# Opening of an attention and gated feed-forward kernel: fewer unread transposes, a later weight load, crossed value loads, an early SiLU table

## The chip, the core and the metric

The kernel runs on one core of a Trainium2 chip. The metric is the device time of one execution in microseconds (us), lower is better. The engines are TensorE (PE, with its weight loads PEld), VectorE (DVE), ScalarE (ACT), GpSimd (POOL) and SyncE (SP), whose queue issues nearly all loads and stores.

## What is computed

`q`, `k`, `v` are 8 batches x 8 heads x 576 rows x 64 columns in float32. Attention runs inside chunks of 64 rows; its result, 4608 tokens x 512, goes through a gated feed-forward layer with 1536 inner columns.

```python
scores = scale * np.matmul(q_c, k_c.transpose(0, 1, 2, 4, 3))   # chunks of 64 x 64
attn = np.exp(scores - max); attn = attn / (sum + 1e-09)
x = (attn @ v_c) as 4608 x 512
g = x @ w_gate
out = (silu(g) * (x @ w_val)) @ w_out
```

## The kernel before, in words

The 4608 tokens are nine blocks of 512. Products in the feed-forward part are made of three passes: each operand is split into a high part (`fp32r`) and a rest, and low x high, high x low and high x high are added in PSUM. The weights are split on the way in: a float64-looking pair of words (`raw`) is turned into `t` by ACT (`scale`, line 84, and `below`, line 91) and DVE (`shift`, `power`, `weigh`, `join`, lines 87 to 102), and then into `w` by `upper` (ACT) and `lower` (DVE). `Up(f)` does so for 128 gate and 128 value columns, `Out(f)` for 128 rows of `w_out`; `wo_raw`, `woh` and `wol` are the latter's results. Up to f = 11 the weights are split while two blocks (0 and 1) are worked on; from block 2 on they are there.

The opening, some 47 us, is attention of blocks 0 and 1, the splitting of weights 0, 1 and 2, and the first feed-forward products. Its order on PE, ACT and DVE is a table of steps written out by hand (`opening`, lines 630 to 637), and no engine departs from its order. A step of attention is a letter, a block, and a head pair or couple: `S` scores (line 228), `M` maxima and `K` their two parts, `B` subtracts the maxima in PSUM by two matmuls (line 585), `E` exponents (line 589), `Z`, `R`, `N` sums, inverses, scaling, `T` transposes on PE (line 392), `C` copies their result to `pT` on ACT (line 608), `X` multiplies by the values (line 406), `U` and `L` split the result into `xh` and `xl`. `G` and `V` are single matmuls of the first products (line 416); `H0` is the SiLU of the first one on ACT (line 434) and `Q0` its product with the other on DVE (line 441). `gs`, `vs`, `w1s`, `w2s` and so on are steps of the weights: `w2s` is `scale` of `Up(2)`. `.6` is six transposes of the identity into a tile that nobody reads (`keep_warm`, line 60); 15 more stand ahead of the table.

The values are needed in two forms: the even head pair of a couple as loaded, the odd one with the two halves of 64 partitions exchanged. `exchange` (line 349) makes the latter on POOL from a loaded tile, for both blocks.

Loads are issued by SP in the order of the program text (lines 507 to 521). A tile of the pool `const` has a tag; two tiles of one tag share their place, so a load into it waits for the last reader of the tile before. A load also waits until the eighth load ahead of it has landed, since its semaphore is used in turn by eight. SP is in order: what is behind a waiting load waits too.

```python
    up[2].load()
    down[0].load()
    values = []
    for a, vs in ((a0, v0), (a1, v1)):
        for c in range(2):
            pool, tag = (ld, "v_t") if a is a0 else (wp, ("woh", "wol")[c])
            odd = pool.tile([P, 2 * T, C], F32, name="v_t", tag=tag)
            a.exchange(vs[c][:, 1], odd)
```

Of the kernel before, what the change touches and what calls it, by code (L numbers as in the profile page):

```python
# [8 lines left out]
F32 = mybir.dt.float32  # L9
# [6 lines left out]
AF = mybir.ActivationFunctionType  # L16
# [3 lines left out]
P = 128  # L20
C = 64
# [6 lines left out]
NP = H // 2  # L28
T = 4
# [6 lines left out]
def attn_then_gated_ffn(ctx: ExitStack, tc: tile.TileContext, qk, v, wgv, wo, out):  # L36
    nc = tc.nc
    const = ctx.enter_context(tc.tile_pool(name="const", bufs=1))
    ld = ctx.enter_context(tc.tile_pool(name="ld", bufs=2))
    one = ctx.enter_context(tc.tile_pool(name="one", bufs=1))  # L40
    wp = ctx.enter_context(tc.tile_pool(name="wp", bufs=2))
    hp = ctx.enter_context(tc.tile_pool(name="hp", bufs=2))
    xs = ctx.enter_context(tc.tile_pool(name="xs", bufs=2))
    small = ctx.enter_context(tc.tile_pool(name="small", bufs=2))
# [6 lines left out]
    ident = const.tile([P, P], F32, name="ident")  # L51
# [4 lines left out]
    def keep_warm(n):  # L56

        ps = ps_gv.tile([P, P], F32, name="unread", tag="ps_gv")
        for _ in range(n):
            nc.tensor.transpose(ps, ident, ident)  # L60
# [44 lines left out]
    class Up(Narrow):  # L105
# [12 lines left out]
        def load(self):  # L118
            f = self.f
            self.raw = const.tile([P, 2 * DM], U64, name="raw", tag=self.at())  # L120
            nc.sync.dma_start(out=self.raw, in_=wgv[f].rearrange("p g n -> p (g n)"))
# [45 lines left out]
    class Out(Narrow):  # L167
# [6 lines left out]
        def load(self):  # L174
            f = self.f
            if f % 2 == 0:
                pool, tag = (const, "w7") if f == 0 else (one, "s_sb")
                Out.raw = pool.tile([P, 2, DM], U64, name="raw", tag=tag)
                nc.sync.dma_start(out=Out.raw, in_=wo[f * P:(f + 2) * P, :].rearrange("(n p) m -> p n m", p=P))
            self.mine = Out.raw[:, f % 2]  # L180
# [144 lines left out]
    class First(Attn):  # L325
# [18 lines left out]
        def load_v(self, p, t):  # L344
            nc.sync.dma_start(out=t, in_=v[:, p:p + t.shape[1], self.b])  # L345

        def exchange(self, t, to):
            for h in range(2):
                nc.gpsimd.tensor_copy(out=to[h * C:(h + 1) * C], in_=t[(1 - h) * C:(2 - h) * C])
# [82 lines left out]
    def silu(pg):  # L432
        h = hp.tile([P, N], F32, name="h")
        nc.scalar.activation(h, pg, AF.Silu, scale=2.0 ** -8)  # L434
        return h
# [4 lines left out]
    def times(h, pv):  # L440
        nc.vector.scalar_tensor_tensor(out=h, in0=pv, scalar=2.0 ** -8, in1=h, op0=ALU.mult, op1=ALU.mult)  # L441
# [49 lines left out]
    up, down = [Up(f) for f in range(NF)], [Out(f) for f in range(NF)]  # L491
# [12 lines left out]
    a0, a1 = First(0), First(1)  # L504
# [2 lines left out]
    w, o = up[0], down[0]  # L507
    q0 = [a0.load_qk(0), a0.load_qk(1)]
    wg = Half(w, 0)
    q0 = q0, [a0.load_qk(2, 2, const, "w4")]  # L510
    v0 = const.tile([P, NP, 2 * T, C], F32, name="v_t", tag="w3")
    v0 = [v0[:, p:p + 2] for p in (0, 2)]
    for p in (0, 2):
        a0.load_v(p, v0[p // 2])
# [2 lines left out]
    up[1].load()  # L517
    v1 = [ld.tile([P, 2, 2 * T, C], F32, name="v_t", tag="qk_t") for _ in range(2)]
    for p in (0, 2):
        a1.load_v(p, v1[p // 2])  # L520
    up[2].load()
    down[0].load()
    values = []
    for a, vs in ((a0, v0), (a1, v1)):
        for c in range(2):
            pool, tag = (ld, "v_t") if a is a0 else (wp, ("woh", "wol")[c])
            odd = pool.tile([P, 2 * T, C], F32, name="v_t", tag=tag)
            a.exchange(vs[c][:, 1], odd)
            values.append((vs[c][:, 0], odd))

    def x_of(a, p):
        return [x[:, p % 2] for x in a.x[p // 2]]
# [87 lines left out]
    for a, qs in ((a0, q0[0] + q0[1]), (a1, q1[0] + q1[1])):  # L620
# [6 lines left out]
    weights = {"g": wg, "v": wv, "w1": up[1], "w2": up[2]}  # L627


    opening = """  # L630
        gs S00 S01 .4 M001 M000 K00 gh gp B000 B001 .6 gb S02 gw S03 .6 E000 gj Z000 E001 Z001 M010 M011 K01 R00
        B010 gu B011 .6 N00 E010 E011 Z010 vs Z011 vb T00 vh T01 .6 S11 R01 N01 S10 T02 C00 T03 C01 gl M100 S13
        C03 M101 S12 vp K10 vw B100 B101 C02 vj X01 M111 E100 E101 M110 vu Z100 K11 X00 Z101 w1s U03 vl R10 B111
        U00 U01 L03 E111 B110 G0_31 N10 V0_31 V0_02 G0_01 V0_32 E110 U02 G0_32 L01 Z110 V0_11 Z111 G0_30 L02
        G0_11 w1b R11 V0_01 T11 L00 N11 T10 G0_10 C10 V0_10 w1h G0_21 G0_22 G0_02 V0_21 G0_12 w2s V0_22 V0_30
        V0_20 V0_00 G0_20 V0_12 G0_00 C11 H0 T12 T13 C12 C13 X10 w1p Q0 U11 X11 U10 U12 w1w U13 w1j L10 L11 L12
        L13 w1u
    """
# [1 line left out]
    for do in opening.split():  # L640
        if do[0] == ".":
            keep_warm(int(do[1:]))
        elif do[0] in "gvw":
            getattr(weights[do[:-1]], steps[do[-1]])()
        elif do[0] in "GV":
            if do[0] not in products:
                products[do[0]] = Product(a0, 0, "GV".index(do[0]))
            products[do[0]].add((int(do[3]), int(do[4])))
        elif do == "H0":
            h0 = silu(products["G"].ps)  # L650
        elif do == "Q0":
            times(h0, products["V"].ps)
        else:
            b, i = int(do[1]), int(do[2])
            pairs = do[0] in "STCUL"
            getattr(couples[b, i // 2 if pairs else i], do[0])(i if pairs else int(do[3:] or 0))
# [65 lines left out]
    f, o = NF - 1, down[NF - 1]  # L722
# [6 lines left out]
    nxt = First(2)  # L729
# [17 lines left out]
    z, two, px = {}, {}, {}  # L747
# [4 lines left out]
    def load_v():  # L752
        for p in range(NP):
            two[p] = (hp if p % 2 else ld).tile([P, 2 * T, C], F32, name="v_t", tag="o_sb" if p % 2 else "v_t")
            if p % 2 == 0:
                nc.sync.dma_start(out=two[p], in_=v[:, p, nxt.b])
            else:
                for h in range(2):
                    r, to = slice(h * C, (h + 1) * C), slice((1 - h) * C, (2 - h) * C)
                    nc.sync.dma_start(out=two[p][to], in_=v[r, p, nxt.b])  # L760

    def turn():
        nxt.turned = const.tile([P, NP, N], F32, name="pT", tag="turned")
# [19 lines left out]
    def rest(p):  # L783
        for i in (p, p + 1):
# [4 lines left out]

    extra = {0: lambda: nxt.exponents(0), 1: lambda: (nxt.exponents(2), sums(0)), 2: lambda: nxt.normalize(0, z[0]),  # L790
             3: lambda: (sums(2), load_v()), 4: lambda: nxt.normalize(2, z[2]), 6: turn, 7: lambda: copy(2),
             8: columns, 9: lambda: (first(2), rest(0)), 10: lambda: rest(2)}
    for f in range(NF):
# [5 lines left out]
    def block(a, b):  # L799
        nxt = Attn(b + 1) if b + 1 < NB else None  # L800
        middle, behind = {}, {}
        if nxt:


            kept_v = []

            def scores():
                tiles = [nxt.load_qk(0), nxt.load_qk(1)], [nxt.load_qk(2, 2, const, "turned")]
                ps = nxt.products(tiles[0], pool=ps_gv, tag="ps_gv"), nxt.products(tiles[1])
                nxt.less_top(nxt.take(ps[0], 0), 0)  # L810
                nxt.less_top(ps[1], 2)

            def load_v():
                kept_v.extend(nxt.load_v_crossed(p, "v_t" if p < 2 else "qk_t") for p in range(NP))

            def values():
                nxt.columns_crossed(kept_v[:2], 0, 2, ps_gv, "ps_gv")
                nxt.columns_crossed(kept_v[2:], 2, 2)

            middle = {3: lambda: nxt.exponents(0, NP)}  # L820
            behind = {1: scores, 3: lambda: nxt.normalize(0, NP), 4: lambda: nxt.turn(0, 0), 5: lambda: nxt.turn(0, 1),
                      6: lambda: (nxt.turn(2, 0), load_v()), 7: lambda: nxt.turn(2, 1),
                      8: values, 9: lambda: nxt.ready(0, 2), 10: lambda: nxt.ready(2, 2)}
        for f in range(NF):
            wo_f = []

            def between():
                middle.get(f, lambda: None)()
                wo_f.extend(out_weights(f))

            h = gated(a, f)
            between()
            lag(parts(a, f, h), wo_f)
            behind.get(f, lambda: None)()
        return nxt

    a = nxt
    for b in range(2, NB):
        a = block(a, b)
# [34 lines left out]
```

## Time and profile before

| | |
|---|---|
| median of 3 runs | 952.28 us (952.1 to 952.45) |
| the profiled execution's own time | 952.15 us |
| its span, first to last instruction | 950.4 us |
| busy share of the span | PE 99%, PEld 82%, DVE 51%, ACT 35%, POOL 1% |
| granted TensorE clock | 1.000 of full speed (the level of 2.4 GHz) |
| matmuls | 6299 |

The span is 1.75 us shorter than the time of that execution; the rest lies around it. The page gives busy shares over the whole span, and PE is busy in nearly all of it, so the places where PE is idle are few and lie at the start: its first slice of 23.8 us shows 7 tenths, all later ones 9 or more except the last.

### The profile page before, as it was taken

The numbers are of one execution on the slowest core, as the hardware profiler recorded it, in microseconds if no ns is written. First come the engines' busy times: TensorE is split into PE (matmuls) and PEld (weight loads), VectorE is DVE, ScalarE is ACT, GpSimd is POOL, SyncE is SP. The second block draws the span as 40 slices with busy tenths as digits, with TensorE's granted clock in tenths as the row PEclk, the third lists the DMA queues.
The fourth block names the chain that finished last, engine by engine and source line by source line (L and its number), as shares of the span: only waits on it lengthen the run. The fifth ranks groups of instructions, "written<-read, shape, count | busy, mean of one in ns | idle before, by whom it ended". The sixth has DMA issues, their size and how long they took to land.

```text
span 950.4 us, 14625 instructions
## 1 busy us (share of the span) xinstructions
PE 940.5 (99%) x6299; PEld 778.6 (82%) x6299; DVE 480.4 (51%) x792; ACT 336.3 (35%) x540; POOL 7.0 (1%) x14
## 2 busy tenths in 40 slices
PE   7999999999999999999999999999999999999998
PEld 6888888888888888888888888888888888888886
DVE  7966666574475336632574337533663256432222
ACT  4745444354332333133323233233423342332222
POOL 1100000000000000000000000000000000000000
PEclk9999999999999999999999999999999999999999
DMA  9614332443300230022102030023002210000001
GB/s 363 228 54 155 155 111 99 156 167 112 89 1 1 89 87 3 1 90 67 23 0 90 1 90 1 5 84 90 1 1 89 67 23 1 1 16 29 1 1 44
DMA packets 43936, 63.85 MB, mean 67 GB/s; under 512 B 27488, under 2 KB 27744, under 8 KB 42464
## 3 DMA queue, kind: packets, MB, share of 16 engines
q1 hardware_dynamic: 42144, 59.78, 18.3%
q10 hardware_dynamic: 1728, 3.15, 0.9%
q8 instruction: 49, 0.80, 0.3%
q14 instruction: 15, 0.12, 0.0%
HBM read 50.33 MB, written 12.58 MB: 66 GB/s over the span
## 4 chain that ended last, share of the span: by engine, by line
PE 97%; DMA 2%; SPq 0%; issue 0%; ACT 0%; DVE 0%
PE ps_gv L416 62%; PE ps_o L460 10%; PE ps_o L462 10%; PE ps_o L461 10%; PE ps_a L228 2%; DMA qk_t<-in_qk 2%; PE ps_a L306 1%; PE ps_a L406 1%; PE ps_a L585 0%; PE ps_a L392 0%; DMA out<-o_sb 0%; PE pt L392 0%; SPq L200 0%; SPq L154 0%; SPq L345 0%
## 5 line engine op out<-in xcount | busy, mean ns | idle before, releaser
L416 PE MATMUL ps_gv<-xh,w 128*128 128x512 f32 x1728 | 531.0, 389 | 0.0
L416 PEld LDWEIGHTS ps_gv<-xh,w 128*128 128x128 f32 x1728 | 324.3, 188 | 67.4 <-ACT xh L535 0.2
L416 PE MATMUL ps_gv<-xl,w 128*128 128x512 f32 x864 | 336.1, 391 | 0.0
L441 DVE SCALAR_TENSOR_TENSOR h<-ps_gv,h 128x512 f32<-128x512 f32 x108 | 74.6, 691 | 365.1 <-PE ps_gv L416 357.8
L416 PEld LDWEIGHTS ps_gv<-xl,w 128*128 128x128 f32 x864 | 162.1, 188 | 34.6 <-issue 0.4
L434 ACT ACTIVATE h<-ps_gv 128x512 f32<-128x512 f32 x108 | 64.6, 598 | 313.0 <-PE ps_gv L416 313.0
L460 PE MATMUL ps_o<-woh,hl 128*128 128x512 f32 x432 | 168.4, 390 | 0.0
L461 PE MATMUL ps_o<-wol,hh 128*128 128x512 f32 x432 | 168.1, 389 | 0.0
L462 PE MATMUL ps_o<-woh,hh 128*128 128x512 f32 x432 | 168.1, 389 | 0.0
L64 ACT CAST hh<-h 128x512 fp32r<-128x512 f32 x96 | 59.6, 620 | 182.7 <-DVE h L441 182.7
L461 PEld LDWEIGHTS ps_o<-wol,hh 128*128 128x128 f32 x432 | 81.1, 188 | 16.9
L460 PEld LDWEIGHTS ps_o<-woh,hl 128*128 128x128 f32 x432 | 81.1, 188 | 16.9
L462 PEld LDWEIGHTS ps_o<-woh,hh 128*128 128x128 f32 x432 | 81.1, 188 | 16.8
L293 DVE STREAM_TRANSPOSE turned<-s_sb 32x256 f32<-32x256 f32 x192 | 83.7, 436 | 2.7
L65 DVE TENSOR_TENSOR wol<-wo,woh 128x512 fp32r<-128x512 f32 x108 | 73.8, 684 | 12.7 <-ACT woh L64 12.6
L65 DVE TENSOR_TENSOR hl<-h,hh 128x512 fp32r<-128x512 f32 x96 | 66.4, 692 | 18.1 <-ACT hh L64 11.1
L64 ACT CAST woh<-wo 128x512 fp32r<-128x512 f32 x108 | 66.1, 612 | 15.9 <-DVE wo L102 15.9
L228 PEld LDWEIGHTS ps_a<-qk_t 64*64 64x64 f32 x1152 | 18.0, 135 | 5.4 <-issue 3.4
L228 PE MATMUL ps_a<-qk_t 64*64 64x64 f32 x1152 | 19.8, 220 | 1.6 <-DMA qk_t<-in_qk 1.6
L99 DVE TENSOR_TENSOR t<-t 128x1024 bf16<-128x1024 bf16 (+1 forms) x13 | 8.5, 650 | 22.1 <-ACT t L91 21.9
L475 ACT ACTIVATE o_sb<-ps_o 128x512 f32<-128x512 f32 (+1 forms) x36 | 18.6, 593 | 2.2 <-PE ps_o L462 2.0
L136 ACT CAST w<-t 128x1024 fp32r<-128x1024 f32 x11 | 11.6, 1054 | 16.7 <-DVE t L102 16.7
(70 smaller groups left out, 409.1 us busy)
## 6 DMA issues: line engine op xcount, KB each, us to landing
raw<-in_wgv SPq DMA_DIRECT2D x11, 1024.0 KB, 7.0
qk_t<-in_qk SPq DMA_DIRECT2D x10, 1024.0 KB, 7.5
out<-o_sb SPq DMA_DIRECT2D x35, 256.0 KB, 2.3
qk_t<-in_qk SPq DMA_DIRECT2D x16, 512.0 KB, 4.0
raw<-in_wo SPq DMA_DIRECT2D x6, 1024.0 KB, 4.9
v_t<-in_v SPq DMA_DIRECT2D x28, 128.0 KB, 2.7
h<-h ACTq DMA_DIRECT2D x12, 256.0 KB, 2.0
h_in<-h SPq DMA_DIRECT2D x6, 512.0 KB, 3.5
```

Of the source, the lines that this page charges most:

```text
L64: nc.scalar.copy(out=hi, in_=src)
L65: (engine or nc.vector).tensor_tensor(out=lo, in0=src, in1=hi.bitcast(F32), op=ALU.subtract)
L136: nc.scalar.copy(out=self.w[:, 0], in_=self.t)
L228: nc.tensor.matmul(ps[h][j * C:(j + 1) * C, i, u // 2, :], part[:, us:us + C], part[:, M * P + us:M * P + us + C], start=not more or first ...
L293: nc.vector.transpose(out=self.turned[to:to + 32, p:p + 2, j, :, 32 * (i % 2):32 * (i % 2) + 32], in_=src[32 * i:32 * i + 32, :, o // 2, 3 ...
L416: nc.tensor.matmul(ps, w, x, start=first and (k, i) == which[0], stop=last and (k, i) == which[-1])
L434: nc.scalar.activation(h, pg, AF.Silu, scale=2.0 ** -8)
L441: nc.vector.scalar_tensor_tensor(out=h, in0=pv, scalar=2.0 ** -8, in1=h, op0=ALU.mult, op1=ALU.mult)
L460: nc.tensor.matmul(o, hl[:, ts], woh, start=f == 0, stop=False)
L461: nc.tensor.matmul(o, hh[:, ts], wol, start=False, stop=False)
L462: nc.tensor.matmul(o, hh[:, ts], woh, start=False, stop=f == NF - 1)
L475: nc.scalar.activation(o_sb[:, m], o[:, m], AF.Copy, scale=2.0 ** -8)
```

## The change

It touches the opening alone.

- `.6` after `B000 B001` and after `S03` become `.2`; `.6` after `B011` and after `T01` go: 20 transposes fewer. 15 and 4 stay ahead.
- The first output weights (`Out(0)` and `Out(1)` in one load) are loaded into the place `w4` instead of `w7`. `w4` holds the values of block 0 now, and the second half of block 0's queries and keys moves from `w4` to `w3`.
- That load stands ahead of the load of `Up(2)` now, not behind it.
- The odd values of block 1 are loaded crossed, as two halves of 64 partitions, straight into their place; POOL's four copies for block 1 go. The four for block 0 stay.
- After `G0_10` (step `*`) ACT does a SiLU of one column of the identity into a tile that nobody reads. Nothing of the result changes.

```diff
-                pool, tag = (const, "w7") if f == 0 else (one, "s_sb")
+                pool, tag = (const, "w4") if f == 0 else (one, "s_sb")
...
+        def load_v_exchanged(self, p, t):
+            for h in range(2):
+                nc.sync.dma_start(out=t[(1 - h) * C:(2 - h) * C], in_=v[h * C:(h + 1) * C, p, self.b])
...
-    q0 = q0, [a0.load_qk(2, 2, const, "w4")]
-    v0 = const.tile([P, NP, 2 * T, C], F32, name="v_t", tag="w3")
+    q0 = q0, [a0.load_qk(2, 2, const, "w3")]
+    v0 = const.tile([P, NP, 2 * T, C], F32, name="v_t", tag="w4")
...
     for p in (0, 2):
-        a1.load_v(p, v1[p // 2])
+        a1.load_v(p, v1[p // 2][:, :1])
+        a1.load_v_exchanged(p + 1, v1[p // 2][:, 1])
+    down[0].load()
     up[2].load()
-    down[0].load()
...
+        elif do == "*":
+
+            nc.scalar.activation(small.tile([P, 1], F32, name="unread"), ident[:, :1], AF.Silu)
```

SP's queue from the load of `Up(1)` on, before (`raw<-in_wgv` is an `Up`, `raw<-in_wo` an `Out` pair, `v_t` the values of block 1; in brackets the semaphores that an issue waits for):

```order
9 L121 DMA raw_128<-in_wgv 128x1024 [waits DMAHW1_49]
10 L345 DMA v_t_130<-in_v 128x2x512 [waits DMAHW2_49,PE_49]
11 L345 DMA v_t_131<-in_v 128x2x512 [waits DMAHW3_49,PE_49]
12 L121 DMA raw_134<-in_wgv 128x1024 [waits DMAHW4_49]
13 L179 DMA raw_136<-in_wo 128x2x512 [waits DMAHW5_49]
14 L121 DMA raw_715<-in_wgv 128x1024 [waits DMAHW6_49,PE_49,Activation_49]
```

and with the change:

```order
9 L121 DMA raw_128<-in_wgv 128x1024 [waits DMAHW1_49]
10 L346 DMA v_t_130<-in_v 128x512 [waits DMAHW2_49,PE_49]
11 L350 DMA v_t_130<-in_v 64x512 [waits DMAHW3_49]
12 L350 DMA v_t_130<-in_v 64x512 [waits DMAHW4_49]
13 L346 DMA v_t_131<-in_v 128x512 [waits DMAHW5_49,PE_49]
14 L350 DMA v_t_131<-in_v 64x512 [waits DMAHW6_49]
15 L350 DMA v_t_131<-in_v 64x512 [waits DMAHW7_49]
16 L180 DMA raw_138<-in_wo 128x2x512 [waits DMAHW0_49,PE_49,Pool_49]
17 L121 DMA raw_140<-in_wgv 128x1024 [waits DMAHW1_49]
18 L121 DMA raw_693<-in_wgv 128x1024 [waits DMAHW2_49,PE_49,Activation_49]
```

Two loads of values became six, and the load of the first `Out` pair, which waited for an earlier load alone, waits for PE and POOL as well, with the load of `Up(2)` (`raw_140`) behind it.

ACT from `below` of `Up(1)` (L91) to the copies of the last transposes, before (`h<-ps_gv` is `H0`, the `L84` row `w2s`, `pT` the steps `C`):

```order
18 L91 ACTIVATE t<-raw 128x1024
19 L608 COPY pT<-ps_a 128x512
20 L84 ACTIVATE t<-raw 128x1024
21 L608 COPY pT<-ps_a 128x512
22 L434 ACT_TABLE_LOAD
23 L434 ACTIVATE h<-ps_gv 128x512
24 L608 COPY pT<-ps_a 128x512 x2
```

and with the change:

```order
18 L91 ACTIVATE t<-raw 128x1024
19 L651 ACT_TABLE_LOAD
20 L651 ACTIVATE unread<-ident 128x1
21 L613 COPY pT<-ps_a 128x512
22 L84 ACTIVATE t<-raw 128x1024
23 L613 COPY pT<-ps_a 128x512
24 L439 ACTIVATE h<-ps_gv 128x512
25 L613 COPY pT<-ps_a 128x512 x2
```

The table load moved from between `w2s` and `H0` to ahead of both and of the copy; one short activation came with it.

## Rows read from the trace of the kernel before

**Rows 1.** Chain of work that ended last, 0 to 48 us: start, us, what.

```profile
4.70 15.05 DMA qk_t<-in_qk
...
22.61 0.88 issue
23.49 1.84 PE ps_a L406 x106
...
33.97 2.27 PE ps_a L406 x128
36.28 11.21 PE ps_gv L416 x48
```

**Rows 2.** Timeline of PE and PEld: start, us, engine, line, operation, count [idle before, releaser].

```profile
1.36 3.34 PE L60 MATMUL unread<-ident 128*128 128x128 f32 x15 [1.36 <-POOL ident masks.py:199]
...
11.21 0.88 PE L60 MATMUL unread<-ident 128*128 128x128 f32 x6
...
13.10 1.13 PE L585 MATMUL ps_a<-tops,minus 128*128 128x512 f32 x4 [1.02 <-DVE tops L578]
...
15.00 0.86 PEld L392 LDWEIGHTS ps_a<-ident,s_sb 128*128 128x128 f32 x8 [0.36 <-ACT s_sb L589]
...
15.93 0.82 PE L60 MATMUL unread<-ident 128*128 128x128 f32 x6
...
17.34 1.16 PE L228 MATMUL ps_a<-qk_t 64*64 64x64 f32 x64 [0.60 <-DMA qk_t<-in_qk]
```

**Rows 3.** Windows 12 to 14 us: busy PE, PEld, DVE, ACT, POOL; clock; DMA; GB/s.

```profile
12.00:14.00 2.00, 0.98 (x5) 0.82 (x5) 1.86 (x7) 0.17 (x1) 1.13 (x3) 1.00 1.02 410
```

**Rows 4.** Timeline of SP: the load of `Up(2)`, of `Up(3)`, and a later pair.

```profile
11.63 0.77 SPq L121 DMA_DIRECT2D raw<-in_wgv  x1
...
36.31 0.34 SPq L121 DMA_DIRECT2D raw<-in_wgv  x1
...
128.64 0.38 SPq L179 DMA_DIRECT2D raw<-in_wo  x1
129.07 0.46 SPq L121 DMA_DIRECT2D raw<-in_wgv  x1
```

**Rows 5.** DMA issues, us to landing: issued at 10.13, 11.63, 129.07, 36.31, 36.75.

```profile
v_t<-in_v SPq DMA_DIRECT2D x1, 512.0 KB, 14.7
...
raw<-in_wgv SPq DMA_DIRECT2D x1, 1024.0 KB, 15.6
...
raw<-in_wgv SPq DMA_DIRECT2D x1, 1024.0 KB, 6.9
...
raw<-in_wgv SPq DMA_DIRECT2D x1, 1024.0 KB, 5.9
...
raw<-in_wo SPq DMA_DIRECT2D x1, 1024.0 KB, 8.5
```

**Rows 6.** Timeline of ACT, 29 to 36 us.

```profile
29.98 0.59 ACT L608 COPY pT<-ps_a 128x512 f32<-128x512 f32 x1 [1.14 <-PE ps_a L392]
30.46 1.14 ACT L84 ACTIVATE t<-raw 128x1024 f32<-128x1024 f32 x1
31.49 0.59 ACT L608 COPY pT<-ps_a 128x512 f32<-128x512 f32 x1
32.09 1.28 ACT L434 ACT_TABLE_LOAD   x1
33.39 0.60 ACT L434 ACTIVATE h<-ps_gv 128x512 f32<-128x512 f32 x1
33.88 1.07 ACT L608 COPY pT<-ps_a 128x512 f32<-128x512 f32 x2
```

**Rows 7.** DMA queues, 21.0 to 21.2 us: packets, MB, share.

```profile
q8 instruction: 1, 0.02, 29.0%
```

**Rows 8.** Timeline of PEld, 29 to 30 us.

```profile
29.56 0.14 PEld L392 LDWEIGHTS ps_a<-ident,s_sb 128*128 128x128 f32 x1 [0.33 <-issue]
```

**Rows 9.** Timeline of POOL: its copies of block 1's values.

```profile
23.61 3.08 POOL L349 COPY v_t<-v_t 64x512 f32<-64x512 f32 x4 [7.59 <-DMA v_t<-in_v]
```

More of the change, by code (lines that the diff above doesn't have):

```diff
@@ L519, in attn_then_gated_ffn @@
     for p in (0, 2):
-        a1.load_v(p, v1[p // 2])
+        a1.load_v(p, v1[p // 2][:, :1])
+        a1.load_v_exchanged(p + 1, v1[p // 2][:, 1])
+    down[0].load()
     up[2].load()
-    down[0].load()
     values = []
[L524 to L529, printed above, removed]
+    for vs in v0:
+        odd = ld.tile([P, 2 * T, C], F32, name="v_t")
+        a0.exchange(vs[:, 1], odd)
+        values.append((vs[:, 0], odd))
+    values += [(vs[:, 0], vs[:, 1]) for vs in v1]
     def x_of(a, p):
@@ L630, in attn_then_gated_ffn @@
     opening = """
-        gs S00 S01 .4 M001 M000 K00 gh gp B000 B001 .6 gb S02 gw S03 .6 E000 gj Z000 E001 Z001 M010 M011 K01 R00
-        B010 gu B011 .6 N00 E010 E011 Z010 vs Z011 vb T00 vh T01 .6 S11 R01 N01 S10 T02 C00 T03 C01 gl M100 S13
+        gs S00 S01 .4 M001 M000 K00 gh gp B000 B001 .2 gb S02 gw S03 .2 E000 gj Z000 E001 Z001 M010 M011 K01 R00
+        B010 gu B011 N00 E010 E011 Z010 vs Z011 vb T00 vh T01 S11 R01 N01 S10 T02 C00 T03 C01 gl M100 S13
         C03 M101 S12 vp K10 vw B100 B101 C02 vj X01 M111 E100 E101 M110 vu Z100 K11 X00 Z101 w1s U03 vl R10 B111
         U00 U01 L03 E111 B110 G0_31 N10 V0_31 V0_02 G0_01 V0_32 E110 U02 G0_32 L01 Z110 V0_11 Z111 G0_30 L02
-        G0_11 w1b R11 V0_01 T11 L00 N11 T10 G0_10 C10 V0_10 w1h G0_21 G0_22 G0_02 V0_21 G0_12 w2s V0_22 V0_30
+        G0_11 w1b R11 V0_01 T11 L00 N11 T10 G0_10 * C10 V0_10 w1h G0_21 G0_22 G0_02 V0_21 G0_12 w2s V0_22 V0_30
         V0_20 V0_00 G0_20 V0_12 G0_00 C11 H0 T12 T13 C12 C13 X10 w1p Q0 U11 X11 U10 U12 w1w U13 w1j L10 L11 L12
@@ L757, in load_v @@
             else:
-                for h in range(2):
-                    r, to = slice(h * C, (h + 1) * C), slice((1 - h) * C, (2 - h) * C)
-                    nc.sync.dma_start(out=two[p][to], in_=v[r, p, nxt.b])
+                nxt.load_v_exchanged(p, two[p])
     def turn():
```

## The prediction

> **What bounds the kernel now.** I read the chain of waits first, for the opening alone, then the timelines of PE, ACT and SP there, then the landing times of single loads. The page says that PE is busy 99% of the span; the chain says where it isn't. Until 19.75 us the end is set by a transfer, the last queries and keys of block 1, issued at 4.70 [rows 1]. From there the chain is PE's own work, with a break of 0.88 us at 22.61 in the middle of the first `X` step [rows 1], until the 48 feed-forward matmuls from 36.28 on; behind them PE hardly stops until the end of the kernel. So the change can give back at most what PE stands idle ahead of 36.28 us, and whatever it adds there as a wait of PE stays in the time in full, since nothing later has slack to absorb it. PE's last step of the opening, `X10` and `X11`, runs from 33.97 to 36.24 [rows 1]: the sum below is the shift of its end.
>
> **The transposes.** Of the four places two are shown, and the other two are alike. The six that start at 11.21 end at 12.09, and the next matmul starts at 13.10 and waited 1.02 us for DVE; the six that start at 15.93 end at 16.75, and the next waited 0.60 us for a load [rows 2]. Those ahead of the transposes of 15.00 are alike: PE's weight loads there waited 0.36 us more for the scaled exponents [rows 2]; and the first six stand before a wait for a load too. What PE does less there it waits more. Worth nothing in itself: 0.
>
> What they may have done is keep the clock up. The granted clock is 1.00 of 2.4 GHz in the emptiest stretch, where PE was busy 0.98 of 2 us [rows 3]. With the change the real work between 11.5 and 17.3 us is 1.13 us of `B` and 0.86 us of `T`, some 2.0 of 5.8 us, where three times six transposes at 0.82 to 0.88 came on top [rows 2], 4.5 in all. No row shows how little keeps it up, so it is a rival, and here it costs 0. The Trainium skill speaks against the edit ("TensorE: Matmul & The Clock Gate", "HAM oscillation"): a PE that waits for loads between short bursts falls back to 1.2 GHz and starts each burst cold. By that rule the result is the clock rival below.
>
> **The break at 22.61.** PE's instructions come in packets of a queue of their own; one starts in the window 21.0 to 21.2 us [rows 7], when the load queue is full, and PE stops in mid-step at 22.61 and goes on at 23.49 [rows 1]. I read the break as a wait for that packet. A smaller one, 0.33 us, stands at 29.56 [rows 8]. With 20 transposes fewer PE has 40 instructions fewer ahead of the packet's end, so the break falls 20 matmuls later in the step: if it ends at the same time, 20 x 1.84/106 = 0.35 us of work are done before it instead of behind it. But the packet may be asked for as much later as PE is behind: then nothing is won. Bounds 0 and -0.35, I take the middle, **-0.2**; outside of them it could go altogether (-0.88), a rival. The Trainium skill ("Runtime: NRT & Kernel Launch", "Instruction fetch mechanics") has such refills mostly hidden; then the break is something else and this term is 0, the sum 953.2.
>
> **The crossed loads.** POOL's four copies end at 23.61 + 3.08 = 26.69 [rows 9]; the values are first read by `X10` at 33.97 [rows 1]. Loaded crossed they come with the last piece of their 1 MB. Its issue waits for the load eight places ahead, block 1's first queries and keys, but until 10.13 + 14.7 = 24.8 us, where the same megabyte landed before [rows 5], the queue is full anyway; 9 us before the reader. 0, and 0 also if they come 5 us later. SP's four extra issues lie in waits that it has. If POOL's 3.08 us held up DVE, DVE gains some part of them between 23.6 and 26.7 us, where the chain shows PE at work and not waiting for it: 0.
>
> **The table load.** It costs 1.28 us at 32.09, and ACT is idle 1.14 us before the copy at 29.98 [rows 6]. Moved there it delays that copy by 1.28 + some 0.2 for the unread SiLU - 1.14 = 0.3 us, and takes 1.3 us out of the way of `H0` and of the two copies `C12`, `C13` that `X11` needs. Alone it would be worth nothing to PE, which waits for neither; it counts in what follows.
>
> **The late loads.** This is the term that decides. Before, `Up(2)` was issued at 11.63 and landed 15.6 us later, at 27.2 [rows 4, 5]; its `w2s` on ACT ran at 30.46 [rows 6]. Now the load of the `Out` pair needs the place of block 0's values, which are read until `X00` ends at 23.49 + 1.84 = 25.33 [rows 1], and `Up(2)` stands behind it on SP.
> - The `Out` pair is issued at 25.33 + 0.07 = 25.40 (0.07 is the step from the end of `X11`, 36.24, to the issue at 36.31 that waits for it [rows 4]). `Up(2)` follows 0.43 later, as at 128.64 and 129.07 [rows 4], at 25.83. In that pair `Up` took 6.9 us to land [rows 5]; so it lands at **32.73**. By that time the loads before are through and nothing else is in the queue. Bounds: 5.9, where it was the first of two, and 8.5, the second of two with a third behind [rows 5]; I take 6.9 because order, sizes and an empty queue are the same.
> - `w2s` starts at about 32.75 instead of 30.46, and ACT stands behind it in order: `C11` 1.03 later (31.49 - 30.46), at 33.78, done 0.59 later, at 34.37. `H0` follows at 34.30 without a table load. From its start to the end of `C13` it was 33.88 + 1.07 - 33.39 = 1.56 [rows 6], so `C13` ends at 35.86.
> - `X10` needs `C11`: 34.45 instead of 33.97, +0.5. `X11` needs `C13`: 35.94, where it was ready to start at 33.97 + 2.27/2 = 35.10: +0.84. The second wait ends last and takes the first one in. So the end of `X11` moves by **+0.85**. The rest of ACT and DVE (`U`, `L`, `Q0`, `Up(1)`'s `upper`) moves by about as much and keeps its order relative to PE.
> - The `Out` pair lands at about 30.3 and is first read near 39: 0.
>
> **Sum.** +0.85 from the late load, -0.2 because `X00` ends earlier and every later time of that chain with it: +0.65 on the profiled execution's 952.15, 952.8. The median of the runs shown is 0.13 above that execution: **953.0 us**.
>
> **Rivals.** A run tells a change of 0.2%, 1.9 us, from none; below 950.4 is faster, above 954.2 slower.
> - *Packets in time.* With less in the load queue from 25 us on, and the packet asked for at another point, the breaks at 22.61 and 29.56 shrink or go. With the first gone, all of the chain is 0.88 us earlier, and the loads too: 952.3 with the wait for `w2s` at 6.9 us; with 5.9 `w2s` is no longer late (24.95 + 5.9 = 30.85, `C13` done at 33.95, `X11` ready at 34.2), the break at 29.56 can count too, and it is 951.3. For it: the break is where no wait stands in the program. Against it: the queue is full until 24.8 either way.
> - *A slow pair.* If `Up(2)` lands as the 8.5 us of the second load at 36.75 [rows 5], 1.6 us later than I take, all of it reaches `X11`: 953.0 + 1.6 = 954.6, slower. The point from which it decides is a landing past 33.9 us. Against it: there a third load was queued at once behind, here nothing is.
> - *The clock.* If TensorE falls to 1.2 GHz between 12 and 20 us, `S`, `B` and `X` from 19.88 to 25.33 stretch. The price: the first 15 transposes took 3.34/15 = 0.22 us each, the six at 11.21 0.88/6 = 0.15 [rows 2]; at up to twice the time for the 4.5 us of work there, +2 to +4.5, so 955 to 957.5, say 956.2. It decides as soon as one stretch from 17 us on shows a granted clock below 1.
> - *The wait isn't there.* If the place were free earlier, `Up(2)` would be issued near 18 us and land by 30; the sum is -0.2 and the loss 0: 952.1. Against it: the issue order lists PE among what that load waits for.
>
> **How the numbers follow.** Forecast 0.56, between 952.2 and 953.6; packets in time 0.17; slow pair 0.12; clock 0.11; no wait 0.04. Faster by over 0.2% would need more than all PE breaks of the opening after 20 us, 0.88 + 0.33 and what is left of smaller ones: 0.03. Slower: the clock, most of the slow pair, a sliver of the forecast: 0.2. Within: 0.77. The range takes in the packets' 951.3 and the slow pair and stops short of most of the clock: 951.2 to 955.2.
>
> **What would show it.** Right: in the profile after, ACT waits about 2 us for `raw` ahead of the line-84 operation near 32.7 us; PE waits for `pT` copies of ACT before and within the second pair of `X` steps, a bit over 1 us together; the first 48 feed-forward matmuls start near 36.9; POOL has four copies; granted clock 1.00 throughout; landing of `Up(2)` near 7 us. The break in `X` some 20 matmuls later. Wrong: `w2s` without a wait, or a granted clock of 0.5 anywhere before 40 us; a start of the queries' and keys' matmuls other than 19.9 us would mean that the loads ahead aren't served in order.

## The result, and the profile after

The kernel with the change takes 953.95 us (median of 21 runs, 953.08 to 957.77), the kernel before 952.45 (21 runs, 951.96 to 953.18). The medians differ by 1.5 us; the ratio formed from all runs is 1.0020, with a 95% interval of 1.0013 to 1.0026. So the change makes the kernel slower, by about 0.2%. The forecast was 953.0 in 951.2 to 955.2. The profiled execution took 954.22, 2.07 more than that of before.

| | before | after |
|---|---|---|
| span | 950.4 us | 952.4 us |
| mean granted clock | 1.000 | 0.998 |
| matmuls | 6299 | 6279 |
| end of `X00` | 25.33 | 26.77 |
| landing of `Up(2)` | 27.2 | 34.2 |
| start of the 48 feed-forward matmuls | 36.28 | 38.45 |

The chain of work that ended last, of the kernel after (start, us, what):

```profile
19.24 1.58 PE ps_a L397 x8
20.82 1.92 PE ps_a L229 x64
22.73 1.19 PE ps_a L590 x4
23.92 0.84 PE ps_a L411 x42
24.76 0.50 issue
25.26 1.50 PE ps_a L411 x86
...
34.27 0.89 PE ps_a L397 x8
35.16 0.06 issue
35.22 0.57 ACT pT L613
35.79 0.50 ACT h L439
36.29 0.97 ACT pT L613 x2
37.26 0.04 issue
37.30 1.15 PE ps_a L411 x60
38.45 11.12 PE ps_gv L421 x48
```

and the same view of before, the rows between those of [rows 1]:

```profile
19.88 1.16 PE ps_a L228 x64
21.04 1.06 PE ps_a L585 x4
22.10 0.50 PE ps_a L406 x22
```

In the profiled execution the feed-forward matmuls start 2.17 us later, which accounts for all of its 2.07 us. It falls in two parts, parted by the end of `X00`: 1.44 ahead of it, 0.73 behind. Behind it the chain runs over ACT where before it was PE's own work: this is the forecast's late load. ACT's timeline after shows it:

```profile
30.37 1.28 ACT L651 ACT_TABLE_LOAD   x1
31.66 0.20 ACT L651 ACTIVATE unread<-ident 128x1 f32<-128x1 f32 x1
31.78 0.57 ACT L613 COPY pT<-ps_a 128x512 f32<-128x512 f32 x1
34.17 1.15 ACT L84 ACTIVATE t<-raw 128x1024 f32<-128x1024 f32 x1 [1.83 <-DMA raw<-in_wgv]
35.22 0.57 ACT L613 COPY pT<-ps_a 128x512 f32<-128x512 f32 x1
35.68 0.60 ACT L439 ACTIVATE h<-ps_gv 128x512 f32<-128x512 f32 x1
36.17 1.08 ACT L613 COPY pT<-ps_a 128x512 f32<-128x512 f32 x2
```

`w2s`, the L84 row, waits 1.83 us for `Up(2)`; in [rows 6] the same row waits for nothing. The copies for `X10` and `X11` are behind it. SP, and the landings of the two loads issued at 26.82 and 27.25 (the second row merges `Up(2)` with the next load, which waits):

```profile
26.82 0.39 SPq L180 DMA_DIRECT2D raw<-in_wo  x1
27.25 11.60 SPq L121 DMA_DIRECT2D raw<-in_wgv  x2
```

```profile
raw<-in_wo SPq DMA_DIRECT2D x1, 1024.0 KB, 4.9
...
raw<-in_wgv SPq DMA_DIRECT2D x1, 1024.0 KB, 6.9
```

Ahead of `X00`'s end the chain is PE's own work, slowed. Windows of PE after: length, busy PE, granted clock, DMA share, GB/s:

```profile
16.00:18.00 2.00, 0.18 (x2) 1.00 1.04 430
18.00:20.00 2.00, 1.92 (x70) 0.89 1.03 434
20.00:22.00 2.00, 2.00 (x52) 0.50 1.00 362
22.00:24.00 2.00, 2.00 (x40) 0.76 0.99 242
```

From 16 to 18 us PE waits for queries and keys and does 0.18 us of work, where transposes stood before; then the clock is granted at 0.50, the level of 1.2 GHz, from 19.56 to 22.97. The last scores take 1.92 us instead of 1.16.

### The profile page after: what moved, and what is told of

Same layout as the page of the kernel before. It is cut to its first block, busy times and chain, and to the rows that moved or that the text cites. A ratio compares the mean times of both kernels' runs of the same rounds, so it can differ in the third digit from the quotient of the medians.

```text
span 952.4 us, 14585 instructions
## 1 busy us (share of the span) xinstructions
PE 940.4 (99%) x6279; PEld 778.2 (82%) x6279; DVE 479.7 (50%) x792; ACT 336.2 (35%) x541; POOL 3.5 (0%) x10
## 4 chain that ended last, share of the span: by engine, by line
PE 97%; DMA 2%; SPq 0%; ACT 0%; issue 0%; DVE 0%
PE ps_gv L421 62%; PE ps_o L465 10%; PE ps_o L466 10%; PE ps_o L467 10%; PE ps_a L229 2%; DMA qk_t<-in_qk 1%; PE ps_a L307 1%; PE ps_a L411 1%; PE ps_a L397 0%; PE ps_a L590 0%; DMA out<-o_sb 0%; PE pt L397 0%; ACT pT L613 0%; SPq L346 0%; SPq L201 0%
```

## The experiments

Medians; `before` ran beside each, at 952.2 to 952.3. The ratio is formed from all runs and can differ from that of the medians by up to 0.001. e1, e9 and e10 have five runs, e3 seven, e4 twelve, the others eleven.

| run | edit | us | ratio, 95% interval |
|---|---|---|---|
| e2 | before, 20 transposes fewer | 952.46 | 1.0006 [0.9997, 1.0014] |
| e7 | before, early SiLU | 952.34 | 1.0002 [0.9993, 1.0011] |
| e8 | before, crossed loads | 953.45 | 1.0012 [1.0003, 1.0021] |
| e3 | before, late loads | 954.7 | 1.0027 [1.0016, 1.0037] |
| e4 | after, `Up(2)` ahead of `Out` | 952.94 | 1.0015 [1.0005, 1.0025] |
| e1 | after, all transposes back | 955.88 | 1.0040 [1.0027, 1.0053] |
| e5 | e1, `Up(2)` ahead of `Out` | 952.72 | 1.0005 [0.9996, 1.0014] |
| e6 | e1, work in PE's wait | 954.36 | 1.0022 [1.0013, 1.0031] |
| e9 | after, first two groups of six back | 955.09 | 1.0032 [1.0019, 1.0044] |
| e10 | after, last two groups of six back | 956.64 | 1.0051 [1.0037, 1.0065] |
| e11 | before, `Out` waits, `Up(2)` doesn't; early SiLU | 952.17 | 0.9998 [0.9989, 1.0007] |

**e1: all transposes back.**

```diff
-  ... B000 B001 .2 gb S02 gw S03 .2 ... B011 N00 ... T01 S11
+  ... B000 B001 .6 gb S02 gw S03 .6 ... B011 .6 N00 ... T01 .6 S11
```

> The changed kernel with the 20 unread transposes put back; all else of the change stays. Theory (two costs: the clock falls and holds the end of X00 up by 1.4 us, the late load of Up(2) adds 0.8 us): granted clock 1.000, X00 ends near 25.1 us, Up(2) is issued near 25.6 and w2s waits until about 32.6; the time is that of the kernel before + 0.6, ratio 1.0006. Rival (the late load alone makes the time, the slow stretch lies beside waits): granted clock 1.000, the time unchanged against the changed kernel, ratio 1.0018.

955.88 (954.22 to 956.73). Wrong in sign: with the clock kept up in the opening, the rest of the change costs 3.6 us, more than the 1.5 of the whole change and not less. The profiled execution, 954.22, was the shortest of the five; e1b is a further one.

**e2: fewer transposes alone.** The same edit the other way, in the kernel before.

> The kernel before with the 20 transposes taken out and nothing else. Theory: mean granted clock 0.996 to 0.998 with the fall near 20 us, X00 ends 1.2 to 1.6 us later than in the kernel before, PE doesn't make it up, ratio 1.0013 to 1.0017. Rival: the fall shows, but the waits behind it take it in, ratio 1.000; or no fall at all, then the fall in the changed kernel needs its other edits too.

952.46, no difference that can be told. Yet the clock falls. Windows of PE:

```profile
12.00:14.00 2.00, 0.83 (x2) 0.71 1.04 417
14.00:16.00 2.00, 1.86 (x5) 0.50 1.02 416
16.00:18.00 2.00, 2.00 (x28) 0.50 1.03 424
18.00:20.00 2.00, 2.00 (x60) 0.58 1.04 436
20.00:22.00 2.00, 2.00 (x72) 1.00 1.01 399
```

`B` of 13.17 takes 2.30 us where it took 1.13 [rows 2], but the waits behind it for ACT and for loads [rows 2] take up all but 0.65 us: the last scores start at 20.53 instead of 19.88. The break in `X` then is 0.30 us instead of 0.88, and `X00` ends at 25.39, 0.06 later than before. For the median, a fall that lies between 13 and 20 us is nearly free. One of the eleven runs took 955.89, though; more on such runs at the end of the next section.

**e3: late loads alone.** Of the diff only the exchange of `w4` and `w3` and the load order.

```diff
+    down[0].load()
     up[2].load()
-    down[0].load()
```

> The kernel before with only the places w4 and w3 exchanged as in the change and the Out load ahead of that of Up(2), so that both wait for X00. Theory: granted clock 1.000; w2s waits until 32.7 us, and since the table load still stands ahead of H0, C13 and X11 come 0.85 + 1.28 = 2.1 us later than before: ratio 1.0022. Rival (the load is covered, the change's loss is all clock): ratio 1.000.

954.7. The wait is there at a clock of 1.00, without the rest of the change. ACT:

```profile
33.31 1.17 ACT L84 ACTIVATE t<-raw 128x1024 f32<-128x1024 f32 x1 [2.64 <-DMA raw<-in_wgv]
34.39 0.56 ACT L608 COPY pT<-ps_a 128x512 f32<-128x512 f32 x1
34.97 1.28 ACT L434 ACT_TABLE_LOAD   x1
36.26 0.60 ACT L434 ACTIVATE h<-ps_gv 128x512 f32<-128x512 f32 x1
```

Here the table load stands behind the late `w2s` and adds its 1.28 us to what `X11` waits for.

**e4: the order undone in the change.** The same two lines exchanged back in the kernel after.

> The changed kernel with the load of Up(2) ahead of that of the Out pair again, so that it doesn't wait for X00. Theory: Up(2) is issued near 20 us (when the load eight places ahead has landed) and lands by 28, no wait of w2s; the clock still falls (0.996 to 0.998), the end of X11 is 1.2 to 1.6 us later than before, ratio 1.0014. Rival (the late load alone): ratio 1.000 or below.

952.94, with three of the twelve runs at 956.4 to 956.6. In the profiled execution (952.14) the clock is 0.50 from 13.90 to 17.31, `Up(2)` lands at 29.6, and `w2s` doesn't wait. The ratio's interval overlaps that of the change, so this pair alone doesn't part the order's price; e1 and e5 do.

**e1b: e1, one more execution.**

> The kernel of e1_transposes_back once more, for a profile alone. Its times ran from 954.2 to 956.7, and the one run whose mean granted clock was 1.000 was the fastest. Theory (PE stands for some 2 us before X10 and X11, which wait for w2s behind the late load, and the clock falls there): a stretch of granted clock 0.50 that begins between 34 and 38 us, where the feed-forward matmuls then take up to twice 0.227 us each, time near 956. Rival (the fall is where the transposes are, or the spread is another landing time of Up(2)): a fall before 25 us, or none and a landing after 35 us.

956.45. PE's last step of the opening, and windows of PE there:

```profile
34.55 0.33 PE L411 MATMUL ps_a<-pT,v_t 64*64 64x64 f32 x4
36.84 3.44 PE L411 MATMUL ps_a<-pT,v_t 64*64 64x64 f32 x124 [1.96 <-ACT pT L613]
```

```profile
36.00:38.00 2.00, 1.16 (x64) 0.97 0.00 0
38.00:40.00 2.00, 1.99 (x64) 0.50 0.03 8
40.00:42.00 2.00, 2.00 (x14) 0.68 0.22 49
```

`Up(2)` lands 8.5 us after its issue; PE waits 1.96 us in `X10` for ACT, and about 1 us after it has begun again the clock falls to 0.50, from 37.87 to 41.28. In e1's own profile PE waited 1.92 us and the clock stayed at 1.00; that execution was 2.2 us shorter.

**e5: both undone.** e1 with `Up(2)` ahead of `Out`.

> The changed kernel with the 20 transposes put back and Up(2) loaded ahead of the Out pair: what is left of the change is the crossed loads, the early SiLU table, the place of the Out load and its wait. Theory (all of the loss is Up(2) behind the wait, and the clock behind that): granted clock 1.000, no wait of w2s, ratio 0.999 to 1.000. Rival (the crossed loads cost something themselves, their six issues or their pieces): ratio 1.001 or more.

952.72, clock 0.999 or 1.000 in all eleven runs. Against e1 the order is worth 3.2 us; the two intervals are apart. Without the transposes the same two lines are worth 1.0 us by the medians (e4 against the change). What stays in e5 is within 0.2%.

**e6: the wait filled.** e1 with ten unread transposes between `C13` and `X10`, where PE waits.

```diff
-  ... T12 T13 C12 C13 X10 ...
+  ... T12 T13 C12 C13 ~10 X10 ...
+        elif do[0] == "~":
+            ps = ps_a.tile([P, P], F32, name="unread", tag="ps_a")
+            for _ in range(int(do[1:])):
+                nc.tensor.transpose(ps, ident, ident)
```

> The kernel of e1_transposes_back with ten more unread transposes on PE between T13 and X10, where PE waits for ACT; they write a free bank and need nothing. Theory (the clock falls in that wait): granted clock 1.000 in most runs, times 953 to 954.5, the mode near 956 gone, ratio 1.0010 to 1.0020. Rival (the clock has nothing to do with that wait): median as in e1_transposes_back, ratio 1.003 to 1.004, or later by the ten transposes' 1.2 us.

954.36, clock 0.999 or 1.000 in all eleven runs, where four of e1's five had 0.998; none is above 955.2. `Up(2)` lands as late as in e1 (8.3 us). The two intervals overlap, but four of e1's five runs are longer than all eleven of e6. So the fall behind the late wait is real, and filling that wait takes it away: 1.5 us of median.

**e7: the SiLU alone.** The step `*` in the kernel before.

> The kernel before with the unread SiLU alone. Theory: the table load moves into ACT's idle time ahead of the copy at 30 us, nothing on PE waits for it there, ratio 0.9995 to 1.0003. Rival: H0, which comes 1 us earlier, lets X11 or the first feed-forward matmuls start earlier: 0.5 to 1 us faster, ratio 0.999.

952.34: nothing.

**e8: the crossed loads alone.** `load_v_exchanged` in the kernel before, both load places as they were.

> The kernel before with the crossed loads of block 1's odd values in place of POOL's copies, the load of Up(2) behind them as before. Theory: nothing waits for these values before 34 us; the loads ahead of Up(2) take six places of the eight semaphores, so Up(2) is issued near 18 to 20 us instead of 11.6 and lands by 30, in time for w2s: ratio 0.9995 to 1.0005. Rival: the six pieces slow the queue, queries and keys of block 1 land 0.3 to 0.7 us later than 19.8 and PE with them: ratio 1.0005 or more.

953.45: 1.2 us that the prediction costed at nothing. The chain:

```profile
22.88 0.50 PE ps_a L410 x22
23.38 1.20 issue
24.58 1.84 PE ps_a L410 x106
...
29.80 0.76 PE ps_a L396 x7
30.57 0.58 issue
31.14 0.33 PE ps_a L396
```

Both breaks in PE's own work are longer than in [rows 1] and [rows 8]: 1.20 instead of 0.88, 0.58 instead of 0.33. Windows of the same kernel, then of the kernel before (busy PE, PEld, DVE, ACT, POOL; clock; DMA share; GB/s):

```profile
22.00:24.00 2.00, 1.38 (x26) 0.86 (x25) 2.00 (x4) 1.52 (x3) 0.00 (x0) 1.00 1.08 249
24.00:26.00 2.00, 1.42 (x96) 1.42 (x100) 1.86 (x7) 1.67 (x3) 0.00 (x0) 1.00 1.00 266
```

```profile
22.00:24.00 2.00, 1.12 (x55) 0.95 (x58) 1.90 (x6) 2.00 (x4) 0.40 (x1) 1.00 1.08 428
24.00:26.00 2.00, 2.00 (x91) 1.86 (x82) 1.97 (x5) 1.67 (x4) 1.90 (x3) 1.00 0.99 418
```

The DMA engines are as busy and move 249 and 266 GB/s instead of 428 and 418; from 22 to 24 us a packet of 2048 bytes takes a median of 129 ns instead of 84. It is not the pieces alone: from 24 to 26 us a packet of 8192 bytes of the upward weights beside them takes 495 ns instead of 309. The same bytes hold the queue for longer, and what shares it (the upward weights, PE's instruction packets) comes later. The Trainium skill ("DMA: Bandwidth & Descriptors", "Rules for kernel authors") advises against two transfers to disjoint halves of the partitions, since they share all engines; the trace agrees, as all 16 engines are busy in these windows (shares of 1.08 and 1.00) while the rate falls.

Not all of e8's loss is shown to come from there. In its profile the feed-forward matmuls start 1.60 us later than before; the two breaks make 0.57 of that, and 0.77 is the landing of the last queries and keys (20.52 against 19.75), as its rival had it. But that landing is late in kernels without crossed loads too (e3, e11), and not late in two with them (e4, e5).

**e9, e10: two of the four groups of six at a time.**

> The changed kernel with the first two groups of six transposes put back and the last two left out: 12 fewer than before, not 20. Two theories for the landing of Up(2), which took 8.3 to 8.5 us with all transposes back and 6.9 with 20 fewer. Theory (PE's instruction packet falls on one DMA engine in the middle of that transfer; 24 instructions fewer put it off by some 2.7 us): landing near 7 us, packet after 33 us. Rival (pieces of the values still in flight at the issue make it late): 8.3 to 8.5 as with all back. For the clock: a fall between 13 and 23 us if the last two groups hold it, none there if the first two do.

> The changed kernel with the last two groups put back and the first two cut to two transposes: 8 fewer than before. Theory: the packet is put off by 16 instructions, some 1.8 us, to about 33.6, at the end of the transfer, landing 7 to 8.4. For the clock: no fall before 23 us if the last two groups hold it, and then the fall at the wait behind w2s in some runs, times 953 to 956.

e9 955.09, clock 1.000 in three of five runs; e10 956.64, clock 0.996 or 0.998 in all, and 0.50 from 13.53 to 16.94 in the profile. The first two groups, ahead of 12.1 us, are the ones that mostly hold the clock. Neither kernel is shorter than the change: with 12 and with 8 transposes fewer PE's breaks in `X` are 1.63 and 1.94 us, and `Up(2)` takes 8.1 and 8.4 us to land, in e9 too, where 7 was forecast. So the time doesn't follow the clock of the opening. The start of `X` in e9, then in e10, up to the break:

```profile
22.52 0.72 PE ps_a L411 x34
```

```profile
22.89 0.62 PE ps_a L411 x30
```

**e11: what might beat both.** `Out` waits for its new place, `Up(2)` stays ahead of it, the SiLU is early, nothing is crossed by loads.

> The kernel before with two edits: the first output weights' load waits for the end of the first values, as in the change, but the load of the second upper half of the upward weights stays ahead of it and is issued at about 11.6 us as before; and the unread SiLU. All transposes are kept and the second block's odd queries, keys and values are crossed by TensorE as before. Theory (the crossed loads, not the waiting of the output weights, lengthen TensorE's breaks, and the late landing came from what stood behind the wait): 0.5 MB less stands in the load queue between 20 and 27 us, the breaks at 22.6 and 29.6 us shrink or stay, the upward weights land before 27 us, and the block's end at 36.28 us comes up to 0.7 us earlier: 951.5 us, ratio 0.9993. Rival (nothing is won, since other loads fill the queue): 952.3 us, ratio 1.000. Second rival (the output weights, landing about 31 us, are read earlier than that): an added wait of VectorE or ScalarE and a ratio above 1.001.

952.17, ratio 0.9998: no gain that can be told, and no loss. (Block 1's odd values are exchanged by POOL here, as before, and not by TensorE as that text has it.) The break in `X` is 0.56 us and the second one is gone, but the last queries and keys landed at 20.3 instead of 19.75 in its profile, so `X00` ended no earlier than before. Against e5, which differs by the crossed loads alone, its median is 0.55 us shorter; the two intervals overlap.

## Why the prediction was right, and where it was not

**The late load: right, place and size.** Counted from the end of `X00`, the prediction had the `Out` pair 0.07 us later, `Up(2)` 0.50 later, a landing of 6.9 us, `w2s` at +7.42, `C13` done at +10.53. Measured: 0.05, 0.48, 6.9, +7.40 and +10.48. The term was +0.85; the second half of the shift is 0.73. e3 shows it by itself, e5 takes it away.

**Its price has two more parts that weren't in the sum.** They show in e1, where the late load costs 3.2 us. One is the landing. It was 6.9 to 7.1 us or 8.1 to 8.5, the latter in all five profiles of the change with transposes put back; the rival "slow pair" gave 8.5 a reason, a third load queued behind, that isn't there. What goes with it in all seven profiles is PE's next instruction packet, on its own queue:

| | packet starts, us after the issue of `Up(2)` | landing of `Up(2)`, us |
|---|---|---|
| e6, e10, e1b | 5.5, 5.57, 5.66 | 8.3, 8.4, 8.5 |
| e1, e9 | 5.92, 5.96 | 8.4, 8.1 |
| after, e3 | 6.15, 6.47 | 6.9, 7.1 |

A packet that starts while the load still runs goes ahead of a piece of it. In e1 it starts at 31.79 and takes 0.88 us; the 8 KB that start as it ends take 0.86 instead of 0.31, and the last piece ends 1.2 us behind those of the other fifteen DMA engines. It is so in all five: fifteen engines are through 6.5 to 6.8 us after the issue, as all sixteen are in the change and e3, and one comes 1.1 to 1.4 us behind. In the change the packet starts at 33.40, when the load is nearly through. DMA queues of e1, 31.79 to 31.82 us, and of the kernel after, 33.40 to 33.45 (packets, MB, share):

```profile
q8 instruction: 1, 0.02, 183.1%
```

```profile
q8 instruction: 1, 0.02, 109.9%
```

The rival of e9, values still in flight, falls: in e1b, e9 and e10 they had all landed (26.3 to 26.4) before `Up(2)` was issued (26.7 to 27.6). What moves the packet is less clear. Between the two cases lie 0.2 us of its start, so the 40 instructions fewer of the change can be enough to move it off the load; but e1 and e1b, one kernel, differ by 0.26, and the change's landing is known from one profile. The other part is the clock behind the wait, next.

**The clock: the rival's condition came true, its price did not.** "Granted clock 1.00 throughout" is wrong: every run of the change has 0.996 to 0.998. The six-transpose groups do keep the clock up. The term was put at 0 beside [rows 3], 0.98 us of work in 2 at a clock of 1.00; in the change 0.18 us were left in the two from 16 us on. But e2 shows a fall at a price of 0.06 us in `X00`'s end, because waits for ACT and loads cover most of it and a shorter break the rest. Where it lies decides. In the change's profile it comes late, behind the long wait of 16 to 18 us, and stretches the last scores by 0.76 us and the `B` steps behind them by 0.13 (1.92 - 1.16 and 1.19 - 1.06); by e6 a fall behind the late wait costs 1.5 us of median. The Trainium skill's rule on short bursts between waits for loads ("TensorE: Matmul & The Clock Gate", "HAM oscillation") told the fall rightly; by that rule alone e1 would have been the shorter kernel, and it is 1.9 us longer.

**The break at 22.61: right in itself, wrong as the shift of `X00`'s end.** PE stops after 22 matmuls of `X` with all transposes, after 30, 34 and 42 with 8, 12 and 20 fewer (e10, e9, the change): one matmul later for each transpose left out, so the stop keeps its place among PE's instructions. The packet starts near the end of the last scores in both kernels, at 21.08 before and at 22.53 after, so these 20 matmuls are done between its start and the stop. `X` with its break takes 2.85 us instead of 3.23: 0.38 less, near the bound -0.35 and not the bound 0. This is one pair of profiles, and breaks vary by more: 0.62, 1.04 and 1.33 us in e1, e6 and e1b, which have the same instructions up to there.

The step that failed is the one from there to the sum: -0.2 stood for the whole shift of `X00`'s end, and that came 1.44 later. The last scores start 0.94 later (20.82 against 19.88), +0.76 and +0.13 come from the clock, -0.38 from the break: 1.45. Of the 0.94, 0.72 is the landing of the last queries and keys (20.47 against 19.75), the rest the stretched transposes before the scores. The prediction had named another start of these scores than 19.9 as a sign of being wrong. That landing lies between 19.70 and 20.52 over all profiles, with the crossed loads (e4, e5: 19.9; e8: 20.5) and without (e7: 19.7; e3, e11: 20.3 to 20.4); what sets it stays open. The Trainium skill's sentence that such refills are mostly hidden ("Runtime: NRT & Kernel Launch", "Instruction fetch mechanics") fits the execution as a whole, 49 such packets with PE busy 99% of the span, but not this one: PE stands still in `X` for 0.30 to 1.94 us in every profile, and goes on 2.2 to 2.9 us after a packet starts.

**The crossed loads: mis-sized.** Costed at 0 because their reader is 9 us away. The reader was never late; the queue was. Alone they cost 1.2 us (e8), of which the late queries and keys may be a part, and 0.55 against e11, where the intervals overlap.

**The SiLU and the table load: right.** 0 alone (e7), and in e3, without it, 1.28 us stand in the way of `X11`.

So the term that decided was right, and what stood beside it was not. Ahead of `X00`'s end the sum was 1.64 us short (-0.2 against +1.44): the profiled execution came out 1.4 us above its 952.8, the median 1.0 above its 953.0. That the time still lay in the range is in part luck. The landing of 6.9, chosen for order, sizes and an empty queue, holds only where the packet just misses the load; with the 8.1 to 8.5 of five other profiles the time would by estimate have been 1.2 to 1.6 us longer, at or past the range's end of 955.2.

Still open: three of the change's 21 runs (956.8 to 957.8), three of e4's twelve and one of e2's eleven are some 3 to 4 us longer than the others; none of them was profiled. All seven are of kernels with 20 transposes fewer and a clock of 0.996 to 0.998. None of the 44 runs of e5, e7, e8 and e11, which have all transposes and no late `Up(2)`, is above 954.2. So the transposes may guard against such runs, at no gain for the median.

## What to carry to other kernels

Price a moved load by who stands behind its wait in the issuing queue, and follow that load to its first reader on an in-order engine: here this gave place and size. A transfer with a far-off reader still isn't free when the queue is full: while pieces of 64 partitions moved, all packets took longer, and what shared the queue, instruction packets too, came later. Work that only keeps the clock up is worth what the stretch behind it can't hide, so look for where the fall would lie and what waits there, not only whether it falls.

## What the runs showed of the hardware

- PE's clock fell to 0.50 behind a wait of about 2 us: at 19.56 us, after the wait that ended at 18.08 in the change, and at 37.87, after the one that ended at 36.84 in e1b. It doesn't always: e1's profile shows the latter wait and a clock of 1.00.
- PE stood still in mid-step for 0.30 to 1.94 us while an instruction packet of 16 KB shared the DMA engines with the loads, and went on 2.3 to 2.9 us after the packet's start in the nine profiles with crossed loads, against 2.2 to 2.4 us in the five without them. The stop came at the same place among PE's instructions whatever was left out ahead of it.
- One such packet on one of 16 DMA engines made a load of 1 MB land 8.1 to 8.5 us after its issue instead of 6.9 to 7.1; the other fifteen were through at the same time.
- With loads of 64 partitions in the queue, busy DMA engines moved 249 to 266 GB/s instead of 418 to 428, and packets of other loads took longer too (495 ns instead of 309 for 8192 bytes).
